# Attention in chunks of 64 tokens on quarters of the TensorE array, with VectorE turning q and k

## The chip, the cores and the metric

The kernel runs on one core of a Trainium2 chip. The metric is the device time of one execution in microseconds (us), as the median of several executions. A core has five engines with queues of their own: TensorE (PE in the profile; its weight loads have a row of their own, PEld), VectorE (DVE), ScalarE (ACT), GpSimd (POOL) and SyncE (SP, which issues all of this kernel's DMAs). TensorE reads its operands from SBUF and writes to PSUM, which the other engines empty.

## The reference

First a retention layer (causal attention with a decay and without softmax), then an MLP with a PReLU. There are 8 batches, 8 heads, 576 tokens and 64 features a head; the MLP sees the 4608 tokens with 512 features and has 2048 hidden ones.

```python
scores = q @ k.T / sqrt(64)
gamma = 1 - 2.0 ** (-5 - head)
D = where(i >= j, gamma ** (i - j), 0)       # i, j: token positions
x = (scores * D) @ v                         # (8, 8, 576, 64) -> (4608, 512)
h = x @ w_in
out = (max(h, 0) + alpha * min(h, 0)) @ w_out
```

q, k and v are 32-bit floats. The weights w_in and w_out arrive as 64-bit floats and are brought to 32 bits on the chip.

## The kernel before, in words

**Attention.** A step handles one pair: two heads of one batch, 2 x 64 features, which fill the 128 partitions. There are 8 x 4 = 32 pairs, in the order of the batches. The 576 tokens are cut into NJ = 6 chunks of C = 96. The decay is split into a factor on q and one on v (tables tab, of powers of gamma by position), so that within a chunk only a triangular 0/1 mask is left, and everything from earlier chunks comes through a running sum of k^T v. For pair n the function calls are:

- load_pair (L71-L79) issues six DMAs on SP, two a tensor, one pair ahead, into buffers of which there are two a tensor.
- transposes (L389-L404): GpSimd scales q and v in place (L391). TensorE turns k and q, chunk by chunk, into PSUM (pt, L400), and ScalarE copies the result to kT and qT (L403): features on partitions, tokens along them.
- scores (L406-L417), called twice, for three chunks each: k q^T for each chunk and head (ps, L412), 64 rows by 96 columns, the two heads in the upper and the lower half of the array's rows. VectorE applies the mask on the way to at (L415).
- states (L419-L431): k^T v of the first five chunks (pu, L423), the two heads in the two halves of the array's columns. VectorE makes the running sums su (L426, L428), and ScalarE puts them into sums (L431), a 128x128 tile per chunk with zeros off the two heads' blocks.
- values (L433-L445): v^T at within the chunks (pv, L437), plus sums against qT (pv, L441). put_x (L376-L385) lets ScalarE copy the result to xb, the MLP's input (L384).

All PSUM tiles of the attention (pt, ps, pu, pv) share one tag with two buffers, each one bank.

**MLP.** The tokens are handled in 18 blocks of 256, each in 8 units. In a unit of blocks 1 to 17, TensorE makes seven products ph (L330; a scheme with seven products of half-size blocks in place of eight), VectorE and ScalarE turn them into the activations g (L336-L352), and TensorE makes seven products po with w_out (L257). The products po of a unit are issued after the products ph of the next one. Block 0 uses plain products (L289, L272). When a block is done, VectorE combines po (out_block, L238-L244), and SP stores the result. GpSimd prepares the input combinations of a block (combine_x, L313).

**Weights.** During the first 8 pairs (n < 2 * NST), load_weights brings in the weights in 32 pieces: a DMA on SP, two ScalarE instructions, three of VectorE and one of GpSimd a piece (L183-L198), and the combinations for the seven products on GpSimd (L203).

**Order.** The main loop writes the order out by hand: in each pair, pop_units issues MLP units of the blocks that are ready, a share of the queue in four cuts around the calls above. The Tile framework draws the waits and may move an instruction ahead within its engine's queue. An fp32 product of TensorE appears in the profile as two matmul instructions, each with its own weight load; below these are called passes. Transposes are single.

## Time and profile before

| | |
|---|---|
| median of three runs | 1159.64 us (1159.57 to 1161.23) |
| the profiled execution | 1160.95 us |
| its span, from the first instruction to the last | 1159.2 us |
| VectorE busy | 749.1 us |
| GpSimd busy | 233.2 us |
| ScalarE busy | 187.9 us |
| granted TensorE clock, mean | 0.995 |

The profile is of one execution; all times in it are counted from the span's start. A group is a line of the kernel with an engine, an operation and a shape; it shows the count, the time in which at least one of the group was running, and the mean length of one in ns. A TensorE pass is longer than the distance between two starts, because passes are pipelined. So the prediction goes by starts. The chain of waits follows the last instruction back to what released it, step by step.

### The profile page before, as it was taken

How to read it: one execution, taken by the hardware profiler on the slowest of the kernel's cores; microseconds unless marked ns; L12 is line 12 of the kernel's file. 1: busy time of each engine (PE TensorE's matmuls, PEld its weight loads, DVE VectorE, ACT ScalarE, POOL GpSimd, SP SyncE). 2: the span in 40 equal slices, each digit the busy share in tenths (PEclk: the TensorE clock that was granted, in tenths of full speed). 3: DMA queues.
4: the chain of work that ended last, by engine and by line, in shares of the span. 5: the costliest groups of instructions: out<-in, count | busy, mean ns of one | idle time of the engine just before them, and what ended most of it. 6: DMA issues, size and time to landing. Idle time of an engine off the chain costs nothing.

```text
span 1159.2 us, 21650 instructions
## 1 busy us (share of the span) xinstructions
PE 1126.1 (97%) x8785; PEld 1004.7 (87%) x8785; DVE 749.1 (65%) x2071; ACT 187.9 (16%) x540; POOL 233.2 (20%) x223
## 2 busy tenths in 40 slices
PE   6878999999999999999999999999999999999998
PEld 5756679999999989999999988988898899999997
DVE  6569745756675666766666666576757565667565
ACT  3435311011011111011011111111111111100000
POOL 4788940110021112021012011110112100101000
PEclk9989999999999999999999999999999999999999
DMA  9546411001011111001011101111111110000000
GB/s 238 170 129 202 130 50 32 29 21 40 12 50 32 32 50 32 29 22 50 12 40 32 49 22 50 32 50 28 44 32 44 27 40 1 14 7 19 1 19 19
DMA packets 125636, 55.94 MB, mean 48 GB/s; under 512 B 114768, under 2 KB 114784, under 8 KB 125536
## 3 DMA queue, kind: packets, MB, share of 16 engines
q1 hardware_dynamic: 125536, 54.55, 17.6%
q8 instruction: 70, 1.15, 0.4%
q14 instruction: 30, 0.25, 0.1%
HBM read 45.10 MB, written 9.44 MB: 47 GB/s over the span
## 4 chain that ended last, share of the span: by engine, by line
PE 88%; DVE 5%; POOL 3%; issue 2%; ACT 1%; DMA 1%; SPq 0%; DVEq 0%; POOLq 0%; ACTq 0%
PE ph L330 36%; PE po L257 34%; PE ps L412 4%; PE pv L441 4%; PE pv L437 3%; PE pt L400 3%; PE pu L423 2%; PE ph L289 2%; PE po L272 2%; DVE wa L190 1%; POOL xt L313 1%; POOL vn L391 1%; DVE wc L194 1%; POOL xb L313 1%; DVE w_in L196 0%
## 5 line engine op out<-in xcount | busy, mean ns | idle before, releaser
L257 PE MATMUL po<-w_out,g 128*128 128x256 f32 x1904 | 433.3, 379 | 0.0
L341 DVE TENSOR_TENSOR g<-ph,g 128x256 f32<-128x256 f32 (+1 forms) x544 | 199.8, 388 | 306.0 <-ACT g L336 171.2
L257 PEld LDWEIGHTS po<-w_out,g 128*128 128x128 f32 x1904 | 351.5, 190 | 42.2
L330 PE MATMUL ph<-xb,w_in 128*128 128x128 f32 x2176 | 308.5, 279 | 0.0
L330 PEld LDWEIGHTS ph<-xb,w_in 128*128 128x128 f32 x2176 | 273.0, 192 | 8.7 <-issue 0.2
L330 PE MATMUL ph<-xt,w_in 128*128 128x128 f32 x1632 | 226.7, 275 | 0.0
L330 PEld LDWEIGHTS ph<-xt,w_in 128*128 128x128 f32 x1632 | 204.1, 192 | 0.0
L352 DVE TENSOR_TENSOR g<-g 128x128 f32<-128x128 f32 x544 | 136.3, 291 | 8.3
L336 ACT COPY g<-ph 128x128 f32<-128x128 f32 x136 | 36.1, 265 | 575.5 <-PE ph L330 560.6
L344 DVE TENSOR_SCALAR g<-g,alpha 128x256 f32<-128x256 f32 x272 | 113.7, 460 | 4.8
L391 POOL TENSOR_TENSOR vn<-vn,tab 96x768 f32<-96x768 f32 x32 | 47.0, 1468 | 277.9 <-DMA vn<-in_v_dram 277.2
L346 DVE SCALAR_TENSOR_TENSOR g<-g 128x512 f32<-128x512 f32 x136 | 100.1, 736 | 4.1
L391 POOL TENSOR_TENSOR qn<-qn,tab 96x768 f32<-96x768 f32 x32 | 47.2, 1477 | 144.0 <-DMA qn<-in_q_dram 139.9
L412 PEld LDWEIGHTS ps<-qT,kT 64*96 64x96 f32 x768 | 47.3, 174 | 24.9 <-issue 12.6
L415 DVE TENSOR_TENSOR at<-ps,mask 96x288 f32<-96x288 f32 x128 | 52.7, 447 | 19.9 <-PE ps L412 19.9
L313 POOL TENSOR_TENSOR xt<-xb,xt 128x256 f32<-128x256 f32 x34 | 28.0, 823 | 170.4 <-ACT xb L384 170.0
L412 PE MATMUL ps<-qT,kT 64*96 64x96 f32 x768 | 58.7, 273 | 2.8 <-DVE at L415 2.1
L384 ACT COPY xb<-pv 128x256 f32<-128x256 f32 (+7 forms) x128 | 29.6, 281 | 132.2 <-PE pv L441 132.2
L313 POOL TENSOR_TENSOR xt<-xb 128x256 f32<-128x256 f32 x17 | 12.3, 726 | 192.0 <-PE ph L330 190.1
L437 PEld LDWEIGHTS pv<-at,vn 96*64 96x64 f32 x768 | 36.9, 148 | 14.3 <-DVE g L352 6.6
L441 PE MATMUL pv<-qT,sums 128*128 128x96 f32 x320 | 47.4, 300 | 0.8 <-ACT sums L431 0.8
L441 PEld LDWEIGHTS pv<-qT,sums 128*128 128x128 f32 x320 | 42.4, 208 | 6.2 <-ACT sums L431 1.8
(71 smaller groups left out, 703.2 us busy)
## 6 DMA issues: line engine op xcount, KB each, us to landing
kn<-in_k_dram SPq DMA_DIRECT2D x64, 144.0 KB, 2.7
qn<-in_q_dram SPq DMA_DIRECT2D x64, 144.0 KB, 2.7
vn<-in_v_dram SPq DMA_DIRECT2D x64, 144.0 KB, 2.6
out_dram<-osb SPq DMA_DIRECT2D x36, 256.0 KB, 2.3
raw<-in_moe_w_out_dram SPq DMA_DIRECT2D x12, 512.0 KB, 4.8
raw<-in_moe_w_in_dram SPq DMA_DIRECT2D x11, 512.0 KB, 4.9
w_in<-in_moe_w_in_dram SPq DMA_DIRECT2D x5, 512.0 KB, 5.7
w_in<-in_moe_w_out_dram SPq DMA_DIRECT2D x4, 512.0 KB, 3.5
```

Source lines behind the costliest of these rows:

```text
L257: nc.tensor.matmul(acc[kb][n // 2][:, n % 2, :], g[:, x, :], w_out[i][:, y, :], start=(i == 0 and n % 2 == 0), stop=(i == NU - 1 and (n % ...
L313: nc.gpsimd.tensor_tensor(out=o, in0=x0, in1=x1, op=ALU.subtract)
L330: nc.tensor.matmul(ph[m][:, o], w_in[i // UST][:, l, cc, f0:f0 + P], r[:, cc], start=(n in (0, 3) and cc == 0), stop=(n in (2, 6) and cc = ...
L341: nc.vector.tensor_tensor(out=o, in0=x0, in1=x1, op=ALU.add)
L344: nc.vector.tensor_scalar(g[:, 4 + 2 * m:6 + 2 * m], g[:, 2 * m:2 * m + 2], 0.0, alpha[:, fc:fc + 1], ALU.min, ALU.mult)
L346: nc.vector.scalar_tensor_tensor(out=g[:, 0:4].rearrange("p x t -> p (x t)"), in0=g[:, 0:4].rearrange("p x t -> p (x t)"), scalar=0.0, in1 ...
L352: nc.vector.tensor_tensor(out=g[:, o, :], in0=g[:, x0, :], in1=g[:, x1, :], op=op)
L391: nc.gpsimd.tensor_tensor(out=t, in0=t, in1=tab[x][0:C, c, :, :, None].to_broadcast([C, NJ, 2, D]), op=ALU.mult)
L412: nc.tensor.matmul(ps[h2][:, j], kT[rows, c0:c0 + C], qT[rows, c0:c0 + C], start=True, stop=True)
L415: nc.vector.tensor_tensor(out=at[h2][:, r * JR:(r + 1) * JR], in0=ps[h2], in1=mask[:, None, :].to_broadcast([C, JR, C]), op=ALU.mult)
L437: nc.tensor.matmul(pv[j // JR][h2 * D:(h2 + 1) * D, j % JR], vn[:, j, h2], at[h2][:, j], start=(j % JR == 0), stop=False, skip_group_check ...
L441: nc.tensor.matmul(pv[j // JR][:, j % JR], sm[:, j - 1], qT[:, j * C:(j + 1) * C], start=False, stop=(j % JR == JR - 1), skip_group_check= ...
```

## The change

Chunks become 64 tokens long (NJ = 9), so that nearly every product of the attention has a 64x64 stationary operand, or one of 128 rows by 64 columns. The operand's partitions and the output's say which quarter of the array it takes.

- The scores of chunks 2m and 2m + 1, of two heads each, go to the four quarters in turn; the last chunk, which has no partner, is computed twice to fill the tile. scores is called once, for all nine chunks.
- The states do the same for eight chunks. values does it within the chunks; the sums against qT are now one product a head, of 128 rows (the other head's rows of sums are zeros) and 64 columns.
- States and values each take both buffers of the attention's PSUM tag.
- For pairs 0 to 7, TensorE still turns k and q, in blocks of 128 tokens. For pairs 8 to 31, q and k are loaded in squares of 32x32 (load_sq, four DMAs a tensor in runs of 128 bytes), GpSimd scales q there by a table tabx, and VectorE turns each of them with one instruction over 128x576. k is loaded a second time in its natural layout for the states. transposes for pair n + 1 is called within pair n, ahead of values.
- The natural loads have 128 tokens on the partitions and take four DMAs a tensor instead of two (load_nat); the scaling of a natural tensor takes two instructions (scale).
- The MLP units are spread over three cuts instead of four, and the tables of the powers of gamma are built in fewer steps.

The diff, cut to its core; of functions that are replaced, only the first removed line stands here:

```diff
-    C = 96
+    C = 64
     NJ = S // C
-    NR = 2
-    JR = NJ // NR
+    NM = (NJ + 1) // 2
+    NB = S // 32
...
-    def load_pair(b, c):
...
+    NEARLY = 2 * NST
+    def load_nat(t, src, b, c):
+        for h2 in range(2):
+            h = 2 * c + h2
+            nc.sync.dma_start(t[:, 0:NM - 1, h2, :],
+                              src[b, h, 0:(NM - 1) * P].rearrange("(m p) d -> p m d", p=P))
+            nc.sync.dma_start(t[0:C, NM - 1, h2, :], src[b, h, (NM - 1) * P:S])
+    def load_sq(t, src, b, c):
+        for a in range(4):
+            f0 = (a % 2) * 32
+            nc.sync.dma_start(
+                t[32 * a:32 * a + 32],
+                src[b, 2 * c + a // 2].rearrange("(n t) d -> t n d", t=32)[:, :, f0:f0 + 32])
+    def load_pair(n):
+        b, c = pairs[n]
+        kn = nat.tile([P, NM, 2, D], FP32, tag="nat_k", name=f"kn_{n}")
+        vn = nat.tile([P, NM, 2, D], FP32, tag="nat_v", name=f"vn_{n}")
+        qx = nat.tile([P, NM, 2, D], FP32, tag="nat_q", name=f"qn_{n}")
+        if n < NEARLY:
+            kx = kn
+            load_nat(kn, k, b, c)
+            load_nat(qx, q, b, c)
+        else:
+            kx = nat.tile([P, NB, 32], FP32, tag="sq_k", name=f"kx_{n}")
+            qx = qx.rearrange("p m h d -> p (m h d)")[:, 0:S].rearrange(
+                "p (n r) -> p n r", r=32)
+            load_sq(kx, k, b, c)
+            load_sq(qx, q, b, c)
+            load_nat(kn, k, b, c)
+        load_nat(vn, v, b, c)
+        return kn, kx, qx, vn
+    loaded = {0: load_pair(0)}
...
+    sm = const.tile([P, NJ - 1, 2, D], FP32, name="sums")
...
+    def scale(t, x, c):
+        for rows, m in ((P, slice(0, NM - 1)), (C, slice(NM - 1, NM))):
+            n = m.stop - m.start
             nc.gpsimd.tensor_tensor(
-                out=t, in0=t, in1=tab[x][0:C, c, :, :, None].to_broadcast([C, NJ, 2, D]),
-                op=ALU.mult)
+                out=t[0:rows, m], in0=t[0:rows, m],
+                in1=tab[x][0:rows, c, m, :, None].to_broadcast([rows, n, 2, D]), op=ALU.mult)
+    def transposes(n):
+        c = pairs[n][1]
+        kn, kx, qx, vn = loaded[n]
         kT = attn.tile([P, S], FP32, tag="kT", name=f"kT_{n}")
         qT = attn.tile([P, S], FP32, tag="qT", bufs=2, name=f"qT_{n}")
-        for src, dst in ((kn, kT), (qn, qT)):
...
+        if n < NEARLY:
+            scale(qx, 0, c)
+            scale(vn, 1, c)
+            for src, dst in ((kn, kT), (qx, qT)):
+                for m0, m1 in ((0, 3), (3, NM)):
+                    w = min(m1 * P, S) - m0 * P
+                    pt = ps_a.tile([P, 3 * P], FP32, tag="psa", name=f"pt{m0}_{n}")
+                    for m in range(m0, m1):
+                        rows = min(P, S - m * P)
+                        nc.tensor.transpose(
+                            pt[:, (m - m0) * P:(m - m0) * P + rows],
+                            src[0:rows, m].rearrange("p h d -> p (h d)"),
+                            ident[0:rows, 0:rows])
+                    nc.scalar.copy(dst[:, m0 * P:m0 * P + w], pt[:, 0:w])
+        else:
+            nc.gpsimd.tensor_tensor(out=qx, in0=qx,
+                                    in1=tabx[:, c, :, None].to_broadcast([P, NB, 32]),
+                                    op=ALU.mult)
+            scale(vn, 1, c)
+            for src, dst in ((kx, kT), (qx, qT)):
+                nc.vector.transpose(dst, src.rearrange("p n r -> p (n r)"))
...
+    def scores(n, kT, qT):
+        at = [attn.tile([P, NM, C], FP32, tag=f"at{h2}", name=f"at{h2}_{n}") for h2 in range(2)]
+        ps = [ps_a.tile([P, NM, C], FP32, tag="psa", name=f"ps{h2}_{n}") for h2 in range(2)]
+        for m in range(NM):
+            for p2 in range(2):
+                j = min(2 * m + p2, NJ - 1)
+                for h2 in range(2):
+                    nc.tensor.matmul(ps[h2][half(p2), m], kT[half(h2), chunk(j)],
+                                     qT[half(h2), chunk(j)], start=True, stop=True)
+        for h2 in range(2):
+            nc.vector.tensor_tensor(out=at[h2], in0=ps[h2],
+                                    in1=mask[:, None, :].to_broadcast([P, NM, C]), op=ALU.mult)
+        return at
+    def states(n, kn, vn):
+        ps = [ps_a.tile([P, NM - 1, D], FP32, tag="psa", name=f"pu{p2}_{n}") for p2 in range(2)]
+        for m in range(NM - 1):
+            for p2 in range(2):
+                for h2 in range(2):
+                    nc.tensor.matmul(ps[p2][half(h2), m], kn[half(p2), m, h2],
+                                     vn[half(p2), m, h2], start=(m == 0), stop=(m == NM - 2),
+                                     skip_group_check=True)
+        su = attn.tile([P, NJ - 1, D], FP32, tag="su", name=f"su_{n}")
+        nc.vector.tensor_copy(su[:, 0], ps[0][:, 0])
+        for j in range(1, NJ - 1):
+            nc.vector.tensor_tensor(out=su[:, j], in0=ps[j % 2][:, j // 2], in1=su[:, j - 1],
+                                    op=ALU.add)
+        for h2 in range(2):
+            nc.scalar.copy(sm[half(h2), :, h2], su[half(h2)])
+    def values(n, vn, qT, at):
+        b, c = pairs[n]
+        pv = [ps_a.tile([P, NM, C], FP32, tag="psa", name=f"pv{p2}_{n}") for p2 in range(2)]
+        for m in range(NM):
+            for p2 in range(2 if 2 * m + 1 < NJ else 1):
+                for h2 in range(2):
+                    nc.tensor.matmul(pv[p2][half(h2), m], vn[half(p2), m, h2],
+                                     at[h2][half(p2), m], start=(m == 0), stop=False,
+                                     skip_group_check=True)
+        for j in range(1, NJ):
             for h2 in range(2):
-                rows, c0 = slice(h2 * D, (h2 + 1) * D), (r * JR + j) * C
...
+                nc.tensor.matmul(pv[j % 2][half(h2), j // 2], sm[:, j - 1, h2],
+                                 qT[:, chunk(j)], start=False, stop=(j >= NJ - 2),
                                  skip_group_check=True)
-        for j in range(1, NJ):
-            nc.tensor.matmul(pv[j // JR][:, j % JR], sm[:, j - 1], qT[:, j * C:(j + 1) * C],
-                             start=False, stop=(j % JR == JR - 1), skip_group_check=True)
-        for r in range(NR):
-            put_x(c, b * S + r * JR * C, JR * C, pv[r].rearrange("p j w -> p (j w)"))
+        for p2 in range(2):
+            put_x(b, c, p2, pv[p2])
+    turned = {}
     for n, (b, c) in enumerate(pairs):
         if n + 1 < len(pairs):
-            loaded[n + 1] = load_pair(*pairs[n + 1])
-        kn, qn, vn = loaded.pop(n)
+            loaded[n + 1] = load_pair(n + 1)
+        kn, _, _, vn = loaded[n]
         share = -(-len(queue) // (NPAIR - c)) if n >= 2 * NST else \
             (0, 0, 0, 0, 2, 2, 1, 1)[n]
-        cuts = [(share + i) // 4 for i in range(4)][::-1]
-        kT, qT = transposes(n, c, kn, qn, vn)
+        cuts = [(share + i) // 3 for i in range(3)][::-1]
+        kT, qT = turned.pop(n) if n in turned else transposes(n)
         if n < 2 * NST:
             load_weights(2)
+        at = scores(n, kT, qT)
         pop_units(cuts[0])
-        at = [attn.tile([C, NJ, C], FP32, tag=f"at{h2}", name=f"at{h2}_{n}") for h2 in range(2)]
-        scores(n, 0, kT, qT, at)
-        pop_units(cuts[1])
-        scores(n, 1, kT, qT, at)
         if n < 2 * NST:
             load_weights(2)
         states(n, kn, vn)
+        pop_units(cuts[1])
+        if NEARLY <= n + 1 < len(pairs):
+            if n + 1 == NEARLY:
+                square_table()
+            turned[n + 1] = transposes(n + 1)
+        values(n, vn, qT, at)
+        del loaded[n]
         pop_units(cuts[2])
-        values(n, b, c, vn, qT, at)
-        pop_units(cuts[3])
         if c == NPAIR - 1:
             enqueue(b)
     pop_units(len(queue))
```

More of the change, by code (lines that the diff above doesn't have):

```diff
@@ L404, in transposes @@
-        return kT, qT
-    def scores(n, r, kT, qT, at):
-        ps = [ps_a.tile([C, JR, C], FP32, tag="psa", name=f"ps{h2}_{n}_{r}")
-              for h2 in range(2)]
-        for j in range(JR):
-            for h2 in range(2):
-                rows, c0 = slice(h2 * D, (h2 + 1) * D), (r * JR + j) * C
-                nc.tensor.matmul(ps[h2][:, j], kT[rows, c0:c0 + C], qT[rows, c0:c0 + C],
-                                 start=True, stop=True)
-        for h2 in range(2):
-            nc.vector.tensor_tensor(
-                out=at[h2][:, r * JR:(r + 1) * JR], in0=ps[h2],
-                in1=mask[:, None, :].to_broadcast([C, JR, C]), op=ALU.mult)
```

108 lines of the change are left out of this document (44 added, 64 removed).

## The prediction, made before the result was known

> **What bounds the kernel now.** I read the page first: the busy times and the chain that ended last.
>
> ```profile
> span 1159.2 us, 21650 instructions
> PE 1126.1 (97%) x8785; PEld 1004.7 (87%) x8785; DVE 749.1 (65%) x2071; ACT 187.9 (16%) x540; POOL 233.2 (20%) x223
> PE 88%; DVE 5%; POOL 3%; issue 2%; ACT 1%; DMA 1%; SPq 0%; DVEq 0%; POOLq 0%; ACTq 0%
> ```
>
> TensorE is busy for 97% of the span and carries 88% of the chain; no other engine comes near. An average hides stages, so the next view is the busy time by stretches, cut where the last product of pair 3, pair 7 and pair 31 (the last) starts in the trace. The columns are PE, PEld, DVE, ACT, POOL.
>
> ```profile
> 0.00:67.60 67.60, 51.36 (x367) 43.60 (x367) 39.33 (x120) 27.39 (x63) 42.41 (x45) 1.00 0.74 201
> 67.60:149.10 81.50, 71.34 (x509) 50.16 (x509) 61.84 (x117) 36.51 (x80) 73.46 (x67) 0.94 0.51 146
> 149.10:997.70 848.60, 846.35 (x6848) 763.60 (x6848) 542.97 (x1531) 115.29 (x367) 109.38 (x101) 1.00 0.13 33
> 997.70:1159.20 161.50, 157.06 (x1067) 147.32 (x1066) 104.96 (x303) 8.72 (x32) 7.93 (x11) 1.00 0.04 14
> ```
>
> Three regimes. Until 149 us, eight pairs and the preparation of the weights run together and nothing is saturated but GpSimd (73.5 of 81.5 us in the second row). From 149 to 998 us, 24 pairs run between the MLP units and TensorE is idle for 2.2 us in all: what leaves TensorE there leaves the time. The last stretch holds no attention.
>
> How much of the middle stretch is attention? In it the order of the work repeats, so I take one round of the chain, pair 19 to pair 20, and look only at the starts of the output products (po).
>
> ```profile
> 597.68 3.02 PE po L257 x14
> ...
> 604.70 3.02 PE po L257 x14
> 607.73 3.12 PE ph L330 x28
> 610.85 3.02 PE po L257 x14
> ...
> 618.81 3.02 PE po L257 x14
> ...
> 634.92 3.02 PE po L257 x14
> ```
>
> A unit with nothing between is 3.12 + 3.02 = 6.14 us. What a gap has beyond whole units was paid for attention, changes of the array's shape included. 604.70 - 597.68 = 7.02: half the scores cost 0.88. 618.81 - 610.85 = 7.96: the other half and the states cost 1.82, so the states 0.94. 634.92 - 618.81 = 16.11, two units: values and transposes 3.83. Together 6.53 us a pair, 157 us over 24 pairs. The timeline of TensorE splits the 3.83 and shows the bursts.
>
> ```profile
> 613.81 0.75 PE L412 MATMUL ps<-qT,kT 64*96 64x96 f32 x12
> 615.35 0.80 PE L423 MATMUL pu<-vn,kn 96*64 96x64 f32 x20
> 618.64 3.19 PE L257 MATMUL po<-w_out,g 128*128 128x256 f32 x14
> 621.76 1.21 PE L437 MATMUL pv<-at,vn 96*64 96x96 f32 x24
> 622.90 1.35 PE L441 MATMUL pv<-qT,sums 128*128 128x96 f32 x10
> 624.09 1.08 PE L330 MATMUL ph<-xb,w_in 128*128 128x128 f32 x8
> 627.25 3.19 PE L257 MATMUL po<-w_out,g 128*128 128x256 f32 x14
> ```
>
> Without values, ph would follow at 618.64 + 3.02 = 621.66; it starts at 624.09, and its 28 passes last 3.16 instead of 3.12. Values cost 2.47, the transposes the other 1.36.
>
> **The price of a pass.** Each fp32 product is two passes (x12 above are six products). By the chain a pass of 128 columns takes 3.12/28 = 0.111 us and one of 256 takes 3.02/14 = 0.216: 0.82 ns a column and 7 ns beside, so 0.059 us for 64 columns and 0.085 for 96. The next rows, from the answers on line 412 and on the tile kn, give one pass its length (the middle number).
>
> ```profile
> L412 PE MATMUL ps<-qT,kT x552: 245/245/321, 209.8 to 988.1; 64*96 64x96 f32 x184
> L423 PE MATMUL pu<-vn,kn x640: 221/222/369, 14.2 to 989.7; 96*64 96x64 f32 x160
> ```
>
> The 20 passes of pu start within 0.80 - 0.22 = 0.58 us; one after another they need 19 x 0.059 = 1.12. The 12 of ps start within 0.51, not 11 x 0.085 = 0.94. So two run at once already, in halves of the rows (scores, 64 rows) and of the columns (states, 64 columns). The work of the bursts is 6 x 0.085 = 0.51, 10 x 0.059 = 0.59 and, for values, 12 x 0.085 + 10 x 0.111 = 2.13; 0.37, 0.35 and 0.34 are left for going into another shape and back.
>
> **The change, TensorE, pairs 8 to 31.** Scores: 20 products, 40 passes of 64 columns; if four run at once, 10 slots of 0.059 = 0.59, and one burst where two were: + 0.37 = 0.96 (was 1.76). States: 32 passes, 8 slots, 0.47 + 0.35 = 0.82 (0.94). Values: 36 passes within the chunks, 9 slots, 0.53; 32 passes against the sums have all 128 rows and half the columns, two at once: 16 slots, 0.95; there is one shape more, so 0.34 + 0.18 (half a round trip); 2.00 (2.47). States now hold both attention banks, so values wait until the running sums have read both; with a unit of 6.14 us between, that is over. Transposes: none (1.36). Sum 3.78 instead of 6.53, saving 2.75 a pair, 66 us over 24. Four at once is the value that no row shows. One end is four (0.059 a slot for four), the other the two of pu and ps; I take four, because the halves run freely both by rows and by columns and quarters combine the two. The Trainium skill, TensorEngine Tiling (Array Packing), section Overview, has four independent tiles of 64x64; no run here shows that yet.
>
> **VectorE, ScalarE, GpSimd.** The first of these rows is from the page, the others from the groups by shape.
>
> ```profile
> L341 DVE TENSOR_TENSOR g<-ph,g 128x256 f32<-128x256 f32 (+1 forms) x544 | 199.8, 388 | 306.0 <-ACT g L336 171.2
> L352 DVE TENSOR_TENSOR g<-g 128x128 f32<-128x128 f32 x544 | 136.3, 291 | 8.3
> L344 DVE TENSOR_SCALAR g<-g,alpha 128x256 f32<-128x256 f32 x272 | 113.7, 460 | 4.8
> L346 DVE SCALAR_TENSOR_TENSOR g<-g 128x512 f32<-128x512 f32 x136 | 100.1, 736 | 4.1
> L415 DVE TENSOR_TENSOR at<-ps,mask 96x288 f32<-96x288 f32 x128 | 52.7, 447 | 19.9 <-PE ps L412 19.9
> L428 DVE TENSOR_TENSOR su<-pu,su 128x64 f32<-128x64 f32 x128 | 28.3, 221 | 3.1
> L391 POOL TENSOR_TENSOR qn<-qn,tab 96x768 f32<-96x768 f32 x32 | 47.2, 1477 | 144.0 <-DMA qn<-in_q_dram 139.9
> ```
>
> A turn of 128x576 has no row. Its nearest by size, 736 ns for 512 columns (L346), scales to 0.83 us; the dearest rate per column, 291 ns for 128 (L352), gives 1.31. I take 0.83, two a pair: 1.7 us. Two masks of 320 columns take 2 x 0.50 instead of 4 x 0.45 (-0.8), the running sums two steps of 0.22 more (+0.4). VectorE gains 1.3 us a pair. By the stretch it has 305.6/24 = 12.7 us idle a pair, 10 after TensorE's gain: hidden on average. Locally: a unit needs 4 x 0.388 (L341) + 4 x 0.291 + 2 x 0.460 + 0.736 = 4.4 us of VectorE in its 6.14, so 1.8 are free; the turns stand between two units with values (2.0 us of TensorE) beside them. They fit, unless an output block falls there too; for that I add 0.1 us a pair, 2.4 us. If the cover went, each microsecond would cost 24. ScalarE loses four copies a pair and is idle anyway. GpSimd multiplies 128x576 and 128x512 plus a small rest where it had twice 96x768 (1.48 us): a little less. Both now stand ahead of values, one pair early, and in front of the next combine_x; their loads have landed by then (below), so they hold nothing up.
>
> **DMA.** Pairs from 8 on issue 16 loads instead of 6, with the squares in 128-byte runs and k twice.
>
> ```profile
> 0.80 0.95 SPq L76 DMA_DIRECT2D kn<-in_k_dram  x2
> ...
> 2.89 1.06 SPq L76 DMA_DIRECT2D vn<-in_v_dram  x2
> 3.99 0.50 SPq L140 DMA_DIRECT2D a<-in_moe_alpha_dram  x1
> ...
> 7.82 1.95 SPq L183 DMA_DIRECT2D raw<-in_moe_w_in_dram  x3
> PE aps L143 <- DMA a<-in_moe_alpha_dram: 7.6, 1, 7.6
> kn<-in_k_dram SPq DMA_DIRECT2D x64, 144.0 KB, 2.7
> ```
>
> An issue takes SP 0.5 us and lands 2.7 us later: 16 need 8 us of a pair of 35 (848.6/24), and the squares, issued first at the pair's start, land within some 7 us, while the turn that needs them comes after three or four units (18 us or more). The DMA share in the middle stretch is 0.13; doubling it leaves room. Nothing added; were the squares late, VectorE would wait in its queue with all of g behind it. The output stores queue behind the same loads, and their buffers alternate.
>
> **Before 149 us.** Each pair has 12 issues instead of 6, 3.1 us more of SP. For pair 0 it is exposed: alpha's load moves from 3.99 to about 7.1, and the last row but one shows TensorE waiting 7.6 us for just that; the raw weights, behind two pairs, move from 7.8 to 14. Against it stands a shorter chain in each pair: one wait for the masks instead of two and shorter bursts, some 1 to 1.5 us for each of pairs 0 to 3 where nothing is saturated. These cancel. Pairs 4 to 7 stand against GpSimd, which gains a few tenths each, and partly against TensorE: -2 us. Bounds for the whole: -8 (full 1.5 each for eight pairs, no exposed issue) to +9 (weights 6 late, start 3 late).
>
> **Sum.** The profiled execution took 1160.95 us (span 1159.2 and 1.75 around it), the median run 1159.64: 1.3 less. 1160.95 - 66 + 2.4 - 2 = 1095.4; for a median run 1094, with 1081 to 1112 for this case (1081: no stalls, the -8, and the added change of shape free, 0.18 x 24; 1112: the +9, and 0.3 us a pair lost at changes of shape).
>
> **Rivals.**
> *Passes are taken no faster than now.* The densest burst, pu, has 0.58/19 = 30 ns between starts; nothing in the trace goes below. If that is a limit of issue, or of two places in the array, 140 passes a pair need 70 slots of 0.059 = 4.14 and 1.24 of shape changes: 5.38, saving 1.15 a pair, 28 us, and 1132 in the end. For: no denser row exists. Against: pu with 64 columns and ps with 96 run at 30 and 46 ns, that is each at half its own pass length, so the array set both, not a common rate. The Trainium skill, TensorE: Matmul & The Clock Gate, section "Wait — 56ns, not 53.3ns?", speaks against the change here: matmuls start no closer than about 25 ns, however few columns. By that the sum would be an estimated 140 x 25 ns + 1.24 = 4.7 a pair, 1117; the trace so far agrees with it and doesn't test it. Chance of the rival, with anything between: 0.28.
> *The turns hold VectorE up.* They sit in its queue ahead of the next g. About 2 x 1.8 us (two units) and 2.0 (values) are free around them, 5.6 us; from there each microsecond stalls TensorE, and beyond 5.6 + 2.75 the pair is slower than before: a turn of 4.2 us or more, 7.2 ns a column. At 5 us each it costs 10 - 8.35 = 1.65 a pair, 40 us: 1199. Against: the dearest rate above is 2.3 ns a column. Chance 0.05.
> *Only one pass at a time in quarters* would make 140 x 0.059 = 8.3 + 1.2: three microseconds a pair more, 1230. Two at once in either direction speaks against it; 0.01. That gains and stalls cancel to within 0.2% (what a measurement of this kernel can hardly tell from no change): 0.02.
>
> **Numbers.** Forecast 0.64, first rival 0.28, the rest 0.08. The range from 1081 to 1134 holds the first two but for their tails. Faster 0.92, same 0.02, slower 0.06.
>
> **What would show it.** In the changed profile: 40 passes of ps starting within 0.6 to 0.7 us (right) or 1.2 (first rival); pairs 3.7 to 3.9 us longer than their units; TensorE still idle for only a few microseconds after 150 us; turns of 0.8 to 1.3 us. Idle TensorE released by VectorE's g, or VectorE waiting for the squares, would make it wrong, as would a start later than 150 us for pair 8.

## The result and the profile after

The changed kernel takes 1096.59 us (median of four runs, 1095.81 to 1097.85); the kernel before took 1159.61 us beside it. The ratio is 0.9456, with a 95% interval of 0.9439 to 0.9472. The profiled execution took 1096.04 us, with a span of 1094.3. Lines are now those of the changed kernel: load_nat L79 and L81, load_sq L88, TensorE's transposes L461, VectorE's turns L472, scores L488, states L500, values L517 (within the chunks) and L522 (against the sums); the MLP's ph is L376 and po L303 (plain ones L335 and L318); the raw weights are loaded in L229, and the first step of their conversion, on ScalarE, is L232.

The page first: span, busy times, the chain by engine.

```profile
span 1094.3 us, 25575 instructions
PE 1052.2 (96%) x10465; PEld 940.9 (86%) x10465; DVE 777.3 (71%) x2160; ACT 162.8 (15%) x492; POOL 224.1 (20%) x264
PE 92%; DVE 3%; SPq 2%; ACT 1%; DMA 1%; issue 1%; POOL 0%; DVEq 0%; POOLq 0%; ACTq 0%
```

TensorE still bounds the kernel, with 1,680 more passes and 74 us less busy time. Next the busy time by stretches, cut at the same places as before (the last product of pairs 3, 7 and 31); the columns are PE, PEld, DVE, ACT, POOL, granted clock, DMA share, GB/s.

```profile
0.00:68.20 68.20, 40.37 (x606) 32.70 (x607) 41.18 (x133) 28.31 (x64) 43.19 (x56) 0.77 0.69 196
68.20:143.90 75.70, 68.53 (x746) 47.93 (x744) 51.43 (x108) 33.63 (x79) 54.28 (x58) 0.92 0.63 163
143.90:932.70 788.80, 786.20 (x8058) 712.93 (x8053) 579.76 (x1616) 91.88 (x315) 118.68 (x140) 1.00 0.21 45
932.70:1094.30 161.60, 157.14 (x1072) 147.32 (x1068) 104.92 (x303) 9.02 (x34) 7.93 (x11) 1.00 0.04 14
```

Against the prediction's table, the middle stretch is 848.6 - 788.8 = 59.8 us shorter, the two before it 149.1 - 143.9 = 5.2, and the last is as it was. Together that is the 65 us of the spans. TensorE idles for 2.6 us in the middle stretch, as little as before.

One round of the chain, from pair 19 to pair 20, shows the bursts.

```profile
581.58 3.02 PE po L303 x14
584.60 0.73 PE pv L517 x36
585.33 1.08 PE pv L522 x32
586.41 3.32 PE ph L376 x28
589.73 3.02 PE po L303 x14
...
595.88 3.02 PE po L303 x14
598.90 0.74 PE ps L488 x40
...
602.97 3.02 PE po L303 x14
...
609.12 3.02 PE po L303 x14
612.14 0.62 PE pu L500 x32
...
616.09 3.02 PE po L303 x14
```

A unit alone is again 595.88 - 589.73 = 6.15 us (6.14 before). From po to po, the scores make it 602.97 - 595.88 = 7.09, so they cost 0.95. The states cost 616.09 - 609.12 - 6.14 = 0.83 and the values 589.73 - 581.58 - 6.14 = 2.01. A part of each cost stands behind the burst: ph takes 3.32 us there instead of 3.12. The sum is 3.79 us a pair. Taken over whole pairs (time from one pair's last value product to the next one's, less 3.12 us for each ph and 3.02 for each po between), pairs 9 to 31 cost 3.78 us each (one of them 3.80), where most of them cost 6.51 before.

The bursts are dense because four passes start almost together. These are the distances in ns between the starts of the 40 passes of the scores, read from the trace (first pass at 598.84 us):

```
7 7 6 87   7 6 7 38   7 7 6 39   6 7 7 38   7 6 7 38   7 7 6 39 ...
```

Four passes on four quarters start within 20 ns. The second four follow 107 ns after the first, and from there on each four starts 58 ns after the four before it. All 40 start within 0.594 us.

The turns, from the groups by shape: count, busy us, mean ns of one, idle time before.

```profile
L472 DVE STREAM_TRANSPOSE qT<-qn 128x576 f32<-128x576 f32 x24 | 18.6, 776 | 28.2 <-PE pv L522 28.2
L472 DVE STREAM_TRANSPOSE kT<-kx 128x576 f32<-128x576 f32 x24 | 18.4, 767 | 0.0
```

A turn takes 0.77 us. VectorE's busy time in the middle stretch rises by (579.76 - 542.97)/24 = 1.5 us a pair, and TensorE waits for it there only once.

That once is in pair 8, the first that is turned by VectorE. It costs 8.04 us instead of 3.78 (6.19 before); below, these 4.3 us are called the stall. Here is the chain there, then TensorE's one wait in the middle stretch, then the busy times from 150 to 160 us (columns as above).

```profile
149.00 0.66 DVE wc L240
...
150.10 0.59 DVE w_out L242
...
152.12 0.60 DVE g L343
...
152.76 5.32 PE ph L335 x16
```

```profile
PE ph L335 <- DVE g L343: 2.6, 1, 2.6
```

```profile
150.00:160.00 10.00, 7.40 (x33) 5.27 (x25) 7.66 (x20) 0.76 (x2) 9.92 (x10) 0.83 0.01 3
```

The last pieces of the weights (wc, w_out) are still being converted, on VectorE and in front of the g for which TensorE waits 2.6 us. The 16 passes of ph behind the wait take 5.32 us instead of 16 x 0.216 = 3.46, with the granted clock at 0.83. Together that is about the 4.3 us.

The last four pieces are late for two reasons that the trace shows. First, SP issues them only at 132.2 to 134.2 us (in the kernel before, at 114.3 to 122.8). These are its issues around them.

```profile
115.16 4.32 SPq L88 DMA_DIRECT2D kx<-in_k_dram  x4
119.57 3.10 SPq L88 DMA_DIRECT2D qn<-in_q_dram  x4
...
132.23 1.00 SPq L229 DMA_DIRECT2D w_in<-in_moe_w_out_dram  x2
133.33 0.86 SPq L229 DMA_DIRECT2D raw<-in_moe_w_out_dram  x2
134.24 4.76 SPq L88 DMA_DIRECT2D kx<-in_k_dram  x4
139.10 4.48 SPq L88 DMA_DIRECT2D qn<-in_q_dram  x4
```

Eight square loads occupy SP for 7.4 and 9.3 us here, about 1 us each, where a natural load takes 0.5 to 0.6. Those of pair 8 stand ahead of the four pieces, those of pair 9 right behind them. Between the two, from 126.1 to 130.0 us, SP also waits for a buffer of v. Second, the pieces have landed at 136.5, 137.9, 139.1 and 142.2 us (read from the trace), but ScalarE, which takes the first step of the conversion, starts on them only at 145.0:

```profile
141.64 1.26 ACT L509 COPY sums<-su 64x512 f32<-64x512 f32 x2 [5.73 <-DVE su L506]
144.02 0.95 ACT L432 COPY xb<-pv 128x64 f32<-128x64 f32 x6 [1.12 <-PE pv L522]
144.99 0.68 ACT L232 ACTIVATE wa<-w_in 128x512 f32<-128x512 f32 x1
```

ScalarE idles for 5.73 us ahead of the sums of pair 7, and three of the pieces land in that time. The program calls load_weights ahead of states, which holds these sums; that the pieces stand behind them in ScalarE's queue is the order that the framework made.

The start of the span is later, as the same view of SP's issues and TensorE's longest wait show.

```profile
7.83 0.58 SPq L186 DMA_DIRECT2D a<-in_moe_alpha_dram  x1
...
15.43 1.91 SPq L229 DMA_DIRECT2D raw<-in_moe_w_in_dram  x3
```

```profile
PE aps L189 <- DMA a<-in_moe_alpha_dram: 9.9, 1, 9.9
```

### The profile page after: what moved, and what is told of

It is laid out like the page before. It is cut to its first block, busy times and chain, and to the rows that moved or that the text cites. A ratio compares the mean times of both kernels' runs of the same rounds, so it can differ in the third digit from the quotient of the medians.

```text
span 1094.3 us, 25575 instructions
## 1 busy us (share of the span) xinstructions
PE 1052.2 (96%) x10465; PEld 940.9 (86%) x10465; DVE 777.3 (71%) x2160; ACT 162.8 (15%) x492; POOL 224.1 (20%) x264
## 3 DMA queue, kind: packets, MB, share of 16 engines
q8 instruction: 83, 1.36, 0.5%
## 4 chain that ended last, share of the span: by engine, by line
PE 92%; DVE 3%; SPq 2%; ACT 1%; DMA 1%; issue 1%; POOL 0%; DVEq 0%; POOLq 0%; ACTq 0%
PE ph L376 40%; PE po L303 37%; PE pv L522 4%; PE ph L335 2%; PE pv L517 2%; PE ps L488 2%; PE po L318 2%; PE pu L500 2%; SPq L79 1%; DVE su L506 1%; SPq L81 1%; PE pt L461 1%; DVE wc L240 1%; DMA raw<-in_moe_w_in_dram 0%; DVE w_out L242 0%
## 5 line engine op out<-in xcount | busy, mean ns | idle before, releaser
L303 PE MATMUL po<-w_out,g 128*128 128x256 f32 x1904 | 433.3, 379 | 0.0
L303 PEld LDWEIGHTS po<-w_out,g 128*128 128x128 f32 x1904 | 351.4, 190 | 42.3 <-DVE osb L289 0.2
L376 PE MATMUL ph<-xb,w_in 128*128 128x128 f32 x2176 | 294.4, 278 | 0.0
L376 PEld LDWEIGHTS ph<-xb,w_in 128*128 128x128 f32 x2176 | 269.5, 192 | 9.0 <-issue 0.7
L376 PE MATMUL ph<-xt,w_in 128*128 128x128 f32 x1632 | 226.7, 275 | 0.0
L376 PEld LDWEIGHTS ph<-xt,w_in 128*128 128x128 f32 x1632 | 204.1, 192 | 0.0
L443 POOL TENSOR_TENSOR vn<-vn,tab 128x512 f32<-128x512 f32 x64 | 46.4, 740 | 353.6 <-DMA vn<-in_v_dram 299.0
L506 DVE TENSOR_TENSOR su<-pu,su 128x64 f32<-128x64 f32 x224 | 49.8, 222 | 9.3 <-PE pu L500 0.5
L509 ACT COPY sums<-su 64x512 f32<-64x512 f32 x64 | 39.4, 616 | 76.4 <-DVE su L506 75.6
L432 ACT COPY xb<-pv 128x128 f32<-128x128 f32 (+1 forms) x176 | 30.0, 269 | 123.9 <-PE pv L522 123.9
L522 PE MATMUL pv<-qT,sums 128*64 128x64 f32 x1024 | 43.2, 240 | 2.2 <-ACT sums L509 2.1
L335 PE MATMUL ph<-xb,w_in 128*128 128x256 f32 x128 | 38.1, 442 | 5.4 <-DVE g L343 3.1
L522 PEld LDWEIGHTS pv<-qT,sums 128*64 128x64 f32 x1024 | 38.1, 151 | 5.1 <-ACT sums L509 2.7
L517 PEld LDWEIGHTS pv<-at,vn 64*64 64x64 f32 x1152 | 24.6, 147 | 20.6 <-issue 18.9
L491 DVE TENSOR_TENSOR at<-ps,mask 128x320 f32<-128x320 f32 x64 | 28.5, 482 | 16.5 <-PE ps L488 16.5
```

The source lines that it names most:

```text
L303: nc.tensor.matmul(acc[kb][n // 2][:, n % 2, :], g[:, x, :], w_out[i][:, y, :], start=(i == 0 and n % 2 == 0), stop=(i == NU - 1 and (n % ...
L335: nc.tensor.matmul(ph[:, x], w_in[i // UST][:, cc // 2 * 2 + x, cc % 2, f0:f0 + P], xb[0][:, cc], start=(cc == 0), stop=(cc == NCC - 1))
L376: nc.tensor.matmul(ph[m][:, o], w_in[i // UST][:, l, cc, f0:f0 + P], r[:, cc], start=(n in (0, 3) and cc == 0), stop=(n in (2, 6) and cc = ...
L443: nc.gpsimd.tensor_tensor(out=t[0:rows, m], in0=t[0:rows, m], in1=tab[x][0:rows, c, m, :, None].to_broadcast([rows, n, 2, D]), op=ALU.mult)
L506: nc.vector.tensor_tensor(out=su[:, j], in0=ps[j % 2][:, j // 2], in1=su[:, j - 1], op=ALU.add)
L509: nc.scalar.copy(sm[half(h2), :, h2], su[half(h2)])
```

## Experiments

The theory: the time went because a quarter of the array is a place of its own. It takes a new pass every 58 ns whatever the others do, so that four quarters in turn do four passes in that time; turning on VectorE is hidden; and what is left to lose lies in SP's issues before pair 9. Rivals: the gain comes from something else in the change (fewer shape changes, transposes gone) and the order over the quarters doesn't matter; there is a common rate of issue; VectorE's turns cost time on the path. All edits are of the changed kernel but one. Every run stands against the kernel before, at 1160.3 to 1161.6 us in these runs. "A late pair" is the cost of one of pairs 9 to 31 beyond its units, as above.

**The order over the quarters.** In two_places, the same products are ordered so that only two quarters alternate (first all even chunks, then all odd ones); in one_place, all products of a quarter come in succession. The scores, for example (the states and the products within the chunks likewise; those against qT stay):

```diff
-        for m in range(NM):
-            for p2 in range(2):
+        for p2 in range(2):                      # two_places
+            for m in range(NM):
...
+        for p2 in range(2):                      # one_place
+            for h2 in range(2):
+                for m in range(NM):
```

> The changed kernel with the same products in another order: within scores, states and the products inside the chunks, first all of one half (chunks of even number, or the upper rows), then all of the other, so that neighbours fall on two quarters only. Theory (a slot of 0.059 us takes four passes because they stand in four quarters): 54 slots become some 54 more, scores 20 instead of 10, states 16 instead of 8, values 18 instead of 9; 27 x 0.059 = 1.6 us a pair more, 38 us over the 24 late pairs and a few more in the early ones: 1135 to 1140 us. Rival (passes are cheap because there are fewer bursts and no transposes, and their order does not matter): 1097 as the changed kernel, within 3 us. Second rival (issue of passes binds at 15 ns each): 1097 too.

> As before, but all passes of one quarter first, then the next quarter: one pass at a time. Theory: 108 passes at 0.059 instead of 27 slots, 81 x 0.059 = 4.8 us a pair more, 115 us over 24 pairs and some in the early ones: 1210 to 1220 us, slower than the kernel before the change (1160), which ran two at once. Rival (order does not matter): 1097.

Measured: two_places 1125.36 us, ratio 0.9705 (0.9687 to 0.9723); one_place 1185.12 us, ratio 1.0214 (1.0192 to 1.0236), slower than the kernel before. The chain of two_places, then that of one_place:

```profile
577.54 1.14 PE ps L488 x38
...
591.18 0.91 PE pu L500 x30
...
604.58 1.02 PE pv L517 x34
```

```profile
592.81 1.70 PE pv L517 x36
...
608.09 1.93 PE ps L488 x40
...
622.52 1.47 PE pu L500 x32
```

The scores take 0.74 us on four quarters, 1.14 on two and 1.93 on one; with states and values, that is 0.98 and 3.01 us a late pair more, which is what the late pairs cost (4.76 and 6.79). So the order alone decides, with the same number of passes and of shapes. Both were expected dearer: 40 passes at 58 ns on one quarter would be 39 x 0.058 = 2.3 us from first to last start, and 1.79 were measured. The starts show why: 58 or 59 ns apart inside a quarter, but around each of the three places where the order goes from one quarter to the next, starts also come 4 to 6 ns apart, so that about three slots are saved at each.

**What sets the 58 ns.** In half_columns, each score product is cut into two of 32 columns with the same stationary operand, over the four quarters in turn (80 passes instead of 40; the 160 in the expectation counts them twice).

```diff
+            for w in range(2):
                 for p2 in range(2):
...
-                    nc.tensor.matmul(ps[h2][half(p2), m], kT[half(h2), chunk(j)],
-                                     qT[half(h2), chunk(j)], start=True, stop=True)
+                        nc.tensor.matmul(ps[h2][half(p2), m, w0], kT[half(h2), chunk(j)],
+                                         qT[half(h2), q0], start=True, stop=True)
```

> The changed kernel with each product of the scores cut into two of 32 columns: 80 passes instead of 40, the same result. It asks what binds once the slots get short. By the price of the prediction (0.82 ns a column and 7 ns beside) a slot of 32 columns takes 0.033 us for four passes, 8 ns each; 20 slots of 0.059 less 10... in all 20 x 2 x 0.033 = 1.3 us instead of 0.59, 0.7 us a pair, 17 us over 24 pairs: 1114. If the weight load of 64 columns sets the slot whatever the moving columns are: 20 slots of 0.059 = 1.2, 0.6 a pair, 14 us: 1111. If issue binds at 15 ns, the densest that the changed kernel shows: 160 x 15 = 2.4 us, 1.8 a pair, 43 us: 1140. At 25 ns: 4.0 us, 82 us: 1179.

Measured: 1112.36 us, ratio 0.9588 (0.9572 to 0.9604); a late pair 4.34 us. A row of its chain:

```profile
606.28 1.30 PE ps L491 x80
```

Half the columns cost as much as whole ones: 80 passes start within 1.150 us, four every 58 ns. That could be the slot of a quarter, or a common rate of 1.150/79 = 14.6 ns a pass. The two give the same mean, so half_one_place asks again with the passes of 32 columns in succession on each quarter (the scores alone).

```diff
+        for p2 in range(2):
+            for h2 in range(2):
+                for m in range(NM):
...
+                    for w in range(2):
```

> Scores alone: 80 passes of 32 columns as in half_columns, but with all passes of one quarter in succession (states and values as in the change). Theory: what held half_columns back is the weight load of the quarter, which sets a slot of 58 ns whatever the moving columns; then 80 passes in succession start 58 ns apart within a quarter, a little less over the three boundaries: about 80 x 0.058 = 4.6 us less some 0.5 to 1 at the boundaries, 3.6 to 4.1 from the first pass to the last, and a late pair of about 3.78 + 3.0 to 3.5 = 6.8 to 7.3 us; 24 x 3.3 = 79 us more than the change, about 1175. Rival: half_columns was held back by a rate of issue of some 15 ns a pass, and a pass of 32 columns takes a quarter for only about 32 x 0.82 + 7 = 33 ns; then the 80 passes take 80 x 0.033 = 2.6 us less the boundaries, 2.0 to 2.4, a late pair of 5.2 to 5.6 us, and about 1135.

Measured: 1228.44 us, ratio 1.0594 (1.0573 to 1.0615). Its chain, and two stretches of it:

```profile
630.25 4.16 PE ps L491 x80
```

```profile
208.50:258.80 50.30, 50.30 (x484) 46.69 (x480) 34.17 (x96) 4.42 (x16) 7.03 (x8) 1.00 0.23 47
258.80:306.10 47.30, 47.30 (x440) 44.02 (x436) 27.72 (x78) 3.78 (x14) 3.42 (x4) 0.93 0.14 26
```

The burst grew by 4.16 - 0.74 = 3.42 us, and its passes start 58 or 59 ns apart inside a quarter, though each moves only 32 columns. So the slot belongs to the place and doesn't come from the moving columns; what is left in a pass that has kept its size is the load of the 64 stationary columns. No run changed these columns alone, but the trace of before has a case in which they differ from the moving ones: the passes of pv against the sums (L441 there), with 128 stationary and 96 moving columns, start 112 ns apart. That is the distance of ph's passes, with 128 of both, and not the 85 of ps, with 96 of both. Where the moving columns are the more (po, 256 on 128), the distance is 216 ns. So in all these rows the slot follows the larger of the two numbers. The Trainium skill, TensorE: Matmul & The Clock Gate, section "LDWEIGHTS (loading the stationary operand)", has the load's time go by the operand's columns and not its rows, 1/1.2 ns each; for 64 columns that is an estimated 53 ns, near the measured 58.

The total came out 53 us above what was expected. The eight early pairs do the same scores and pay too (pair 7 ended at 170.8 us instead of 143.9), which the expectation forgot; and many late pairs took 1.6 or 3.2 us more than their 7.20 in stretches with TensorE busy throughout and a lower granted clock (second row), some 24 us in all. The trace shows beside what the clock fell: between pairs 9 and 31 it has 12 stretches of 3.4 or 6.8 us with a granted clock of 0.5, and each begins 3.1 to 4.9 us after the start of a burst of scores, whose 80 passes take 4.0 us. In one_place, whose bursts of scores are less than half as long, no such stretch lies in these pairs. Why only some of the bursts brought the clock down stays open.

**The price of a change of shape.** In scores_in_two, the late pairs' scores are made in two bursts around one unit.

```diff
         for m in range(NM):
+            if m == 3:
+                pop_units(between)
...
-        at = scores(n, kT, qT)
-        pop_units(cuts[0])
+        between = 1 if n >= NEARLY else 0
+        at = scores(n, kT, qT, between)
+        pop_units(cuts[0] - between)
```

> The changed kernel with the scores of the late pairs cut into two bursts (three fifths and two fifths of the products) around one MLP unit, nothing else changed. Theory (going into the quartered shape and back costs 0.37 us a burst): 0.37 x 24 = 9 us more: 1105 to 1107. Rival (the shape change is free and the 0.37 of before was something else, such as waits of the scores): 1097 to 1099.

Measured: 1107.60 us, ratio 0.9546 (0.9531 to 0.956); a late pair 4.14 us, 0.36 more. One more burst costs 0.36 us with the same passes. Over pairs 9 to 31 that is 8.3 us of the 11; 2.4 more lie in pair 8, which cost 10.4.

**Turning.** In turns_on_tensor, TensorE turns q and k in all pairs (natural loads throughout). In turns_twice, VectorE makes each turn twice.

```diff
-    NEARLY = 2 * NST
+    NEARLY = len(pairs)                              # turns_on_tensor
...
-            for src, dst in ((kx, kT), (qx, qT)):
+            for src, dst in ((kx, kT), (qx, qT), (kx, kT), (qx, qT)):    # turns_twice
```

> The changed kernel with TensorE turning k and q in all 32 pairs, as the changed kernel does in pairs 0 to 7: blocks of 128 tokens, no squares, 12 loads a pair. Theory (the parts add up: removing the transposes from TensorE is worth what they cost there): 8 passes of 0.111 and 2 of 0.059 are 1.0 us a pair, with the waits for ScalarE's copies in between up to 1.4; 24 x 1.0 to 1.4 = 24 to 33 us more: 1121 to 1130. So the quarters alone, with one burst of scores less, would be worth 30 to 39 of the 63 us. Rival (the turns on VectorE and the square loads cost as much elsewhere as they save): 1097 to 1105.

> The changed kernel with each of VectorE's turns made twice, the second onto the same tile: 1.54 us a pair more on VectorE, 37 us in all. Theory (VectorE has 3 to 4 us to spare around the turns): no change in the late pairs, 0 to 2 us in all from pair 8, where TensorE waits: 1096 to 1099. Rival (the cover is thin, and the turns hold up the next g): up to 37 us more; half of it would give 1115.

Measured: turns_on_tensor 1134.02 us, ratio 0.9758 (0.9743 to 0.9773), a late pair 5.46; turns_twice 1097.92 us, ratio 0.9444 (0.9425 to 0.9463), a late pair 3.78. From the chain of turns_on_tensor:

```profile
573.65 0.64 PE pt L461 x5
574.28 0.64 PE ph L376 x4
...
```

Each of the two bursts of five transposes takes 0.64 us, and the four passes of ph behind it 0.64 instead of 4 x 0.111 = 0.45: 1.67 us a pair, more than the 1.0 to 1.4 expected. Its pair 8 cost 5.45 us, without the stall. So the 63 us fall into 37 for turning on VectorE and 26 for the chunks of 64 on quarters with one burst of scores less. This holds for taking the turning away first; the other order wasn't run. A second set of turns, 1.5 us a pair on VectorE, changes nothing: the turns are hidden with room to spare.

**The issues on SP.** Four kernels. alpha_first issues alpha's load ahead of the loads of pair 0. fewer_issues does that, and joins the loads of the last 64 tokens of two heads into one: nine natural loads in an early pair instead of twelve, fourteen loads in a late one. weights_first adds to fewer_issues that the first four pieces of the weights are issued ahead of the loads of pair 1. before_more_issues is the kernel before, with the loads of pairs 0 to 7 cut in two: twelve instead of six.

```diff
+    nc.sync.dma_start(a16, moe_alpha.rearrange("(t p) -> t p", p=P))     # ahead of pair 0
     loaded = {0: load_pair(0)}
...
         for h2 in range(2):
...
-            nc.sync.dma_start(t[0:C, NM - 1, h2, :], src[b, h, (NM - 1) * P:S])
+        nc.sync.dma_start(t[0:C, NM - 1], src[b, 2 * c:2 * c + 2, (NM - 1) * P:S].rearrange(
+            "h p d -> p h d"))
...
+    for i in range(4):                               # weights_first, after the loads of pair 0
+        early[i] = raw_tile(i)
+        nc.sync.dma_start(early[i], pieces[i][0])
```

```diff
-                nc.sync.dma_start(t[:, :, h2, :],    # the kernel before
+                cut = (0, 3, NJ) if (b, c) in pairs[:2 * NST] else (0, NJ)
+                for j0, j1 in zip(cut, cut[1:]):
```

> The changed kernel with only the load of alpha issued first of all; 12 loads an early pair and 16 a late one as in the changed kernel. It parts the 10 us that fewer_issues won. Theory (the number of issues does it, all along the first 150 us and at pair 8): alpha alone starts TensorE some 3 us earlier, but the raw weights are issued at 15.4 as before and pair 8 still waits: 0 to 3 us less, 1094 to 1097. Rival (the gate before TensorE's first work did it all): 1086 to 1088.

> The changed kernel with the last 64 tokens of the two heads in one load instead of two (9 natural loads an early pair instead of 12, 14 loads a late pair instead of 16), and the load of alpha issued first of all. Theory (SP's issues are on the path at the start: alpha's landing gates TensorE's first work, 9.9 us in the changed kernel, and the raw weights' issue at 15.4): first work at about 6 us, raw weights at 12.5; 2 to 4 us less: 1092 to 1095. Rival (the start is covered, since pairs 0 to 3 wait for the weights' conversion anyway): 1096 to 1097.

> As fewer_issues, with the first four raw pieces of the weights also issued ahead of the loads of pair 1. Theory (the weights' landing leads the chain of the first 150 us): raw weights issued at 6 instead of 15.4 us, so the conversion starts 5 to 8 us earlier, and 3 to 7 us less than the changed kernel: 1089 to 1093. Rival (pair 1's loads, now behind 2 MB of weights, become late and give it back): 1094 to 1098.

> The kernel before the change with each load of pairs 0 to 7 cut in two (three chunks each): 12 issues a pair instead of 6, same bytes, nothing else. It measures alone what the prediction priced at 3 us for pair 0, covered afterwards. Theory (issues are on the path of the first 150 us): 5 to 10 us more than the kernel before: 1165 to 1170. Rival, the prediction's own sum (only pair 0's 3 us show): 1161 to 1164. Second rival (covered by the conversion of the weights): 1159 to 1161.

Measured:

| | us | ratio and interval | pair 8 | pair 7 ends |
|---|---|---|---|---|
| the change | 1096.59 | 0.9456 (0.9439 to 0.9472) | 8.04 | 143.9 |
| alpha_first | 1095.37 | 0.9441 (0.9428 to 0.9454) | 8.14 | 142.0 |
| fewer_issues | 1086.16 | 0.9342 (0.9329 to 0.9355) | 3.77 | 143.6 |
| weights_first | 1093.74 | 0.9413 (0.9391 to 0.9435) | 3.77 | 149.9 |
| before_more_issues | 1163.20 | 1.0023 (1.0013 to 1.0033) | 6.19 | 151.4 |

fewer_issues is the best version, 10 us below the change, where 2 to 4 were expected. Its SP queue at the start, its chain at the start of pair 8, and ScalarE's first step on the last four pieces:

```profile
0.80 0.40 SPq L112 DMA_DIRECT2D a<-in_moe_alpha_dram  x1
...
12.20 1.91 SPq L229 DMA_DIRECT2D raw<-in_moe_w_in_dram  x3
```

```profile
143.82 1.06 PE ph L335 x4
144.89 0.74 PE ps L488 x40
```

```profile
128.24 0.70 ACT L232 ACTIVATE wa<-w_in 128x512 f32<-128x512 f32 x1 [0.54 <-DMA w_in<-in_moe_w_out_dram]
```

The weights are issued 3.2 us earlier (12.20 for 15.43), the stall of pair 8 is gone (4.3 us), and pairs 0 to 7, which end at about the same time, have 45.4 us of MLP passes among them instead of 40.5. 4.3 + 4.9 + 0.3 is the 9.5 us between the two spans (1094.3 and 1084.8). Alpha alone gave nothing that the intervals tell apart: pair 0 ends at 19.0 us instead of 24.5, pair 3 only at 67.4 instead of 68.2. In weights_first the conversion got ahead of the attention on VectorE: TensorE waits 27.0 us for the running sums su instead of 8.8, pair 7 ends 6 us later, and 7.6 us went back. Doubling the issues of the kernel before costs 2.6 us (1.5 to 3.8 by the interval), as the prediction's own sum had it and not the 5 to 10 of the theory.

What removed the stall? In fewer_issues the last four pieces are issued 8 us earlier, at 124.4 to 126.4 us, land at 128.2 to 132.7, and ScalarE takes each within 0.1 us of its landing, ahead of the sums of pair 7. The traces sort by that order. Where ScalarE starts on these pieces ahead of the sums (turns_on_tensor, fewer_issues, weights_first), pair 8 costs no more than a late pair. Where it takes them behind (the change, alpha_first, two_places, one_place, half_columns, scores_in_two, turns_twice), pair 8 costs 3 to 7 us more. half_one_place takes them behind too and has next to no stall; its burst of scores, 3.4 us longer, would cover the wait, which wasn't tried. No run changed ScalarE's order alone, so the shares of SP's late issues and of this order aren't separated.

**Turning earlier.** fewer_from_4 is fewer_issues with VectorE turning from pair 4 on.

```diff
-    NEARLY = 2 * NST
+    NEARLY = NST
```

> fewer_issues with VectorE turning from pair 4 on instead of pair 8. Theory (in pairs 4 to 7 TensorE is busy nine tenths, so what leaves it counts): four pairs at 1.7 us, at most 7 us less than fewer_issues, 1079 to 1084. Rival (GpSimd and SP set the pace there, and the squares cost five issues more a pair): 1086 to 1092.

Measured: 1123.63 us, ratio 0.9683 (0.9665 to 0.9701), 37 us slower than fewer_issues. Pairs 6, 7 and 8 cost 18.4, 14.5 and 22.8 us instead of 7.7, 7.2 and 3.8, which are the 37 us; the later ones again 3.78. Two stretches, and TensorE's longest waits from 100 to 208 us:

```profile
120.00:145.00 25.00, 16.06 (x204) 10.63 (x202) 13.74 (x29) 6.92 (x16) 13.56 (x15) 0.79 0.54 126
145.00:185.00 40.00, 25.43 (x236) 17.93 (x237) 23.50 (x53) 9.62 (x21) 20.11 (x19) 0.71 0.45 95
```

```profile
PE pv L517 <- DVE su L506: 6.9, 2, 3.5
PE ph L335 <- POOL w_in L244: 6.2, 3, 4.0
```

No engine is full in these stretches (TensorE 16 of 25 us, VectorE 14, GpSimd 14): each waits for another, and the weights' last pieces come late. A turn that is free beside MLP units isn't free while the weights are prepared. Here too ScalarE started on the last four pieces late, at 170.0 us, where they had landed at 151.4 to 161.4. Whether that, the square loads ahead of the weights on SP or the turns in VectorE's queue began it wasn't separated.

## Why the prediction was right

The forecast was 1094; 1096.6 was measured. By its steps:

- **Four passes at once, 0.059 us a slot for four.** Right, and shown by the order alone (one_place, two_places): a slot measured 58 ns. The bursts were put at 0.96, 0.82 and 2.00 us and measured 0.95, 0.83 and 2.01. The saving was put at 2.75 us a pair and measured 6.51 - 3.78 = 2.73.
- **The first rival, no starts below 30 ns.** It falls: 40 passes start within 594 ns, 15 ns each, and 7 ns inside a four. The Trainium skill, TensorE: Matmul & The Clock Gate, section "Wait — 56ns, not 53.3ns?", has a floor of about 25 ns between starts; here it doesn't hold across four quarters, and the measured 1096.6 stands against the 1117 that it gave. The prediction misread its own trace here: the 30 ns of pu are a mean. Start by start, the passes of pu in the kernel before stand 7, 51, 7, 52 ns apart and those of ps 6, 79, 6, 79 (behind the first two). So rows with starts below 30 ns existed, the trace did not agree with a floor of 25 ns, and part of the chance of 0.28 rested on that misreading. The four independent tiles of 64x64 that the Trainium skill, TensorEngine Tiling (Array Packing), section Overview, has, and that no run had shown, are shown.
- **0.37 us for a change of shape.** Right: one more burst costs 0.36 (scores_in_two).
- **No transposes, 1.36 us.** For this kernel's blocks of 128 tokens they would be 1.68 (turns_on_tensor).
- **Turns of 0.83 us, hidden, with 0.1 us a pair for stalls.** A turn takes 0.77. The 2.4 us for stalls was mis-sized in kind: pairs 9 to 31 lose nothing, and twice the turns lose nothing (turns_twice). VectorE's gain of 1.3 us a pair measured 1.5.
- **"Nothing added" by the loads.** True from pair 9 on. It failed in pair 8, whose 4.3 us the sum doesn't have: the prediction reckoned half a microsecond an issue and a quiet SP, and the square loads of pairs 8 and 9 are issued among the weights, at 1 us each; the last weights were issued 11 to 18 us later than before. It also had no term for ScalarE's queue, in which these weights, landed from 136.5 us on, waited until 145.0. fewer_issues, with fewer loads, removes the stall and has the weights both earlier and ahead in that queue; which of the two did it isn't separated.
- **Before 149 us: -2, with pairs 0 to 3 cancelling.** Twelve loads took 7.0 us (0.80 to 7.83), 3.8 more than the six, where 3.1 were reckoned; the weights moved to 15.4, not 14. Pair 3 ended at 68.2 us (67.6 before), so the first four did about cancel. Pair 7 ended 5.3 us earlier, with 1.7 us less of MLP passes among pairs 0 to 7: -3.6 in all.

By the profiled executions: 1160.95 - 61.5 (attention in pairs 8 to 31, 156.5 to 95.0 us) - 3.6 leaves 1095.9, and 1096.04 were measured. The forecast had -66, +2.4 and -2, 65.6 in all. Two errors stood against each other: 4.3 us in pair 8 for the 2.4 of stalls everywhere, and 1.6 us more gained in the start. That the sum came this close is luck to the extent of these 2 us; the 2.73 us a pair are not.

## What to carry to other kernels

Price small products by place: a quarter of the array takes a pass every 58 ns, with 64 stationary columns, and products in succession should go to different places, since the order alone was worth 89 us here. Put all products of one shape into one burst, at 0.36 us for each burst saved. Count DMA issues by the stage into which they fall: three fewer an early pair and two fewer a late one, with alpha first, were worth 10 us, although the queue is idle most of the time. Then look at the engine that uses what has landed: here ScalarE had the weights' pieces behind copies that were not ready, and the first of them lay there for 8.5 us.

## What the runs showed of the hardware

- Passes on four quarters start 6 to 7 ns apart, in program order over the four; the next one starts 38 ns after the fourth, 58 ns after the first.
- A pass of 32 moving columns holds its quarter as long as one of 64, 58 ns, with 64 stationary columns in both. In the kernel before, passes with 128 stationary and 96 moving columns start 112 ns apart, as those with 128 of both.
- Where the order goes from one quarter to the next, starts come 4 to 6 ns apart and the two runs of passes overlap by about three slots.
- Eight square loads in runs of 128 bytes held SP for 7.4 to 9.3 us while the weights were loaded, about twice as long an issue as a natural load.
- The granted clock of the first 68 us was 0.77 in the change, 1.00 in the kernel before and 0.90 in fewer_issues. What it cost there was not separated from TensorE's waits.
- With 80 passes of scores on one quarter at a time (half_one_place), the granted clock fell to 0.5 for 3.4 or 6.8 us, 12 times in pairs 9 to 31, each time 3.1 to 4.9 us after the start of such a burst.
